# Where the first weight pieces are queued, who computes unit 1's own term, and a rewritten order: one change to a fused RWKV-5 / tanh-shrink kernel

## The chip, the cores and the metric

The kernel runs on one core of a Trainium2 chip. Time is device microseconds of one execution; the figure for a kernel is the median of its runs. A profile of one execution stands beside it: the hardware profiler records every instruction and every transfer. Engines: PE multiplies matrices (PEld loads its weights), DVE works on vectors, ACT evaluates functions and copies with a scale, POOL is the slow general engine, SP only issues transfers. ACT and POOL can issue transfers too.

## The reference

Two stages. The first is a linear recurrence over 768 steps for 4 batch rows and 8 heads of width 48:

```
for t in range(S):
    cur = u * k[t] (outer) v[t]              # the own term of step t
    y[t] = r[t] @ (state + cur)
    state = w * state + k[t] (outer) v[t]
```

The second takes y as x of 3072 x 384 (token by model width) through a dense block:

```
h = x @ w_in            # 384 x 2048
g = h - tanh(h)
out = g @ w_out         # 2048 x 384
```

r, k, v, w, u arrive as 32-bit floats. w_in and w_out arrive as 64-bit floats and are converted to 32 bits on the core, by integer and float operations on their two halves.

## The kernel before

**Units.** The recurrence is cut into 24 units, numbered 0 to 23. A unit is 64 steps of two batch rows, all 8 heads: r, k and v of a unit are six transfers of 96 KB (one per batch row and tensor). PE turns r and k (L656, four 128x128 transposes each), DVE scales them by powers of w out of the same PSUM tile into rT and kT (L660, L665; from the third unit on, kT is copied by ACT, L692), PE forms the products of all pairs of steps (`levels`, L606, `x_ps<-rT,kT`), DVE copies those that lie before the diagonal into `at` (L830), and PE multiplies `at` with v (`yk_ps<-at,vt`) and k with v for the state (`yk_ps<-vt,kw`). ACT copies the result to `xt` (L765); DVE or ACT keep the state (L792, L795). From the third unit on, the state enters by products `yk_ps<-rT,state` ahead of the levels.

**The own term** (the diagonal of `at`) is made in one of two ways. For units with n < OWN, ACT scales kT by w times u (`own_k`, L709, four instructions, needs `w_u` from POOL, L564), PE forms the products `x_ps<-rT,kU` (`own_levels`, 16 rows of PE's list, two matmuls each in the trace), and DVE copies their diagonal into `at` (L821). For the others, DVE multiplies r by k (L696) and by u (L824, needs `ub`), sums over each head (L700), and ACT writes the eight sums on eight diagonals (L704, two groups of four).

**Dense tiles.** Two units make a block of 256 tokens, 12 blocks. A tile is one block times 256 of the 2048 hidden columns: 96 tiles. PE makes h in two halves (L217, 1.29 us each), ACT and DVE turn it into g by five and three instructions (`s`, `th`, `tg`, `sq`, `small`; `g`, `m`, `cp`), and PE multiplies g by w_out: as four products (L254), or, from hidden column 1024 on for the first six blocks and for nearly all of the later ones, as seven half-width products of sums (L307), for which POOL adds parts of g (L290, L292, L294). The first six blocks run over the hidden columns in three passes (4, 4 and 8 groups of 128), so that they can begin with few weights.

**Weights.** The w_in and w_out matrices come in sixteen pieces of 768 KB, at first in the order w_in piece 0, w_in piece 1, w_out 0, w_out 1. A w_in piece is four transfers: two of 48 partition rows (288 KB) and two narrow ones of 16 rows (96 KB). Before the change the wide ones went by SP's queue and the narrow ones by POOL's. A piece is converted by five DVE instructions (L185, L186, L189, L190, L191) with two of ACT in between (L187, L188). The first h needs piece 0 after L191.

**What sets the order.** `lay_out` makes a list of some 2400 tasks (an engine, what must be done before, a cost and a due time). `ORDER`, a string of two-character numbers, then says in which order the tasks are written into the program; each engine executes its own in that order, waiting at an instruction until what it needs is there. Task numbers depend on the list, so another list needs another string. The tile framework adds the semaphore waits, also between two engines that only read one PSUM bank. Each transfer from SP or ACT counts on one of eight semaphores in turn (`DMAHW0` to `DMAHW7` in the rows below): a transfer that is issued eighth after another waits until that one has landed. The string also places filler matmuls (L534, on the identity matrix, results unused) where PE has nothing to do.

Of the kernel before, what the change touches and what calls it, by code (L numbers as in the profile page):

```python
# [34 lines left out]
OWN = 1  # L35
# [10 lines left out]
    "00010J2f2g2h2i2j2k2l2m2n0HbWbX02030K040605bWbWbW2o2q3534363231332r2t0I2s07370A0FbWbX080B0C2u2x2y38392v092w3U0D3C"  # L46
    "3B3V3W2p3A3G0U2z0L3R0M2+3S3T3D2_0N3F3H0V3Y0O3I0T3u3E3J0PbWbX3L3K3b0QbX3c300S3M3v3w3a0R3r3e3N3s3t3d0w3O3f3P3X3Z3g"
    "8D3Q3h3i3k0W0G3_4O3j0X8E0d430Y4P4Q3l4L0Z44404M4N453m8F0a3y463+0b3n413o0c423p3x3z15470ebYbYbY484p0u0E4Z8I4o4q0f8P"
    "4a0g494l0h4b4S4A4V4c0i4U4R4T4B3q4W0j8Q4m4n4C4X5I4v4Y4J5J5K4D8H4F0k4dbZ4e4K0l4I8L8R5F4G4f8G4H5G5H4z8SbZ4w134s8K8J"
    "4g5i8T8M8U4u4E4h8N4+8W4i4x8O8X8V4r4t4_8d4y4j5f505T0m525j5k510n5g5h5U8e0o8Y5L5V0p8p535M5N5W0q6C548g5P6D6E5X0r5O0t"  # L50
    "550s5Q698q5R5m565t6A6B8Z4k5S5A578h5lba5n595u8f5D5Y5p8i5B5v8j5C8a5Z5E5w6d8k8l5q6c6e8c5x5a6Z8m6N8b5o5b0v8n5r6a6b58"
    "145c6J8o6F5s5d6G6H8s6O775y8t6P6Q915z8r5e746R6n5+6o8u8w6I5_6j6K926L7678606p6g8x9D6M6373758v61666q688y6S6f6h676r64"
    "7W8z656T7X7Y9562946U937U98967T7V7H6i6V1D7I6k9E7J970xJ+996W9RJ_K06l6m796X7K0yJx9S6Y9H9F6s9I9J8+JyJz6t9T7A7B7h9G8_"
    "6u9K7L7D9A7C6vKP7EKM9d7F7G7a7i6w129e7j7Z7b906z6x7k9L6_KLKN9B6+7d9VKOKQ726y9WK9707M7l719C9X7N0z9M7cKA9U7O9f9YKu0+"
    "9Z7eKvKw7P9a9rKr7fK29i0_9N7Q1L7g7R9OKsKt9j16K1K3KZ9P177m9Q109h9g9b7n1811197o9l9k9s7p1ELF1F1TKBA17qKRL3LGLH9tKa7t"
    "9c1G7vKb7y9m9v7wA29w1A7u1H7x9z9n9xK61B9uLI9o9pLl9yA41CA5AFA3A81e1hKC1MLJLK1fAG1N9q1WKSKTA6KW1U1VAR1OA91g9+1PASAH"
    "1QAI9_A7L4AUAAA0AKAJAVANABKcAM1RALAfKD1SAgAT1I1xADLmLnAWAOACLoAYAjLpLqAZAiArAh7SAmAkAsAXL5AEAaB31iAv1jAtMAAP1J1k"
    "AnAwB41KAlAuAz1pAQAxAyM9MBB6AoBFA+B7LT1lBGBAB51mBTBH1nBIBJAb1XB81YMfB91oAcMgMh1ZBM2G2H1aBBBU2FBCBKBfAeBNBV1bBYBg"
    "Ad1cBXBWApBiBaBL1dAqBh1qBk2324KxA_1r26Bb251sKyKzBOB01t2E1yB1BjBt1z1u1+BuBm1_1vBZC3B2Bv1wByBDBcBw2P20BxC4BlB+BzBn"
    "BE27C5B_BP28Bo2921CH2AC82BBQC9C0C7CIC6BSBRCBBdCJCACM22BeCLCK2XCNCOCTKd2CBp2D2QBqCP2RCUBs2SCC2TChLzL+N4CWBrCXCiN3"  # L60
    "N52UCVCY2IC1CZCaCj2VCtCm2WCkC2CQCbClCDCnCpCoCE2JCq2KCuCF2LCGCcCRCw2MCvCyD52NCz2OCxD62YCS2ZD8C+D92aCdDCD7CeDACf2b"
    "DBDKCg2cDL7rC_DZD0DMDNDDDODa2dDP2eCrDbDRDcDe89CsDQDEDSD1DdDFDgDGDoDT85DUDp86DHEEDqDVDrDsEFDtDvDf87D2Du88EH81ETD3"
    "LUEUDhD4EGDwDIDiEVDxEJDjDJEIEKELDXDkEX8ADlEYEiEWDyEZEaDWEj8BDz8CD+ExEMEyENEbEmDYElEcE+82EkDmEpEOEn83E_FNEqEzF0Eo"
    "FOF3LVErDnFP84FQD_F2FSEd7sE1EeFRE0E2F1E3EPE4ERFTEQE5E6E7ESFVFUFcF4FdF5EsEgFgEtFeEfFfEhFhFjFrFiE8FWE9FsEBEAFkFXFl"
    "EvFuECFt7zFYFwG4FvEDFyFZG5F6FzEuEwG8F7FxGWFmG6F+G9FnF8G7GAGBFAGCF9FBFCGXF_FDGDG0GlGZFEFFFoGYFGGbFaFKGa7+Fb7_FHFp"
    "GeGE80GmFMGdFLFqGFGnFIGpG+GGGoG1GqFJGcG_GfG2GtH2GgGsH1GrG3H5GhH0GiGHGJH3GKGIGLH4GMHDGNGOGQHEGPGTH6HfK5HFH7HGGuGj"
# [328 lines left out]
def near(ctx, tc, r, k, v, w, u, out, shared, moe_w_in, moe_w_out):  # L395
# [3 lines left out]
    V, A, T, G, Q = nc.vector, nc.scalar, nc.tensor, nc.gpsimd, nc.sync  # L399
# [140 lines left out]
    def lay_out(early, across_by):  # L540
# [46 lines left out]
        for n in range(weights.count):  # L587

            queues, data = (("SP",), (3.0,)) if n % 4 > 1 else (("SP", "POOL") * 2, (1.2, .95) * 2)
            of = [add(e, .55, lambda n=n, i=i, e=e: weights.load(n, i, e_of[e]), [converted[n - 4] if n >= 4 else None],  # L590
                      data=x, gated=True) for i, (e, x) in enumerate(zip(queues, data))]
# [688 lines left out]
```

## Time and profile before

| | |
|---|---|
| median of 3 runs | 583.96 us (582.51 to 585.50) |
| profiled execution, its own time | 582.57 us |
| its span (first to last instruction) | 580.8 us |
| granted TensorE clock, mean | 0.998 |
| PE / DVE / ACT / POOL busy | 562.5 / 429.9 / 404.3 / 199.9 us |
| filler matmuls in PE's busy time | 13.5 us, all before 45.4 us |

Times in the rows are from the start of the span. A timeline row has start, busy time (us), engine, line of the program, operation, `out<-in`, count, and in brackets how long the engine had been idle before and what released it. `SPq`, `ACTq` and `POOLq` are the engines' issue queues. A windows row has the stretch, its length, then for each engine busy time (and instructions that began), then clock, share of the transfer engines and GB/s.

### The profile page before, as it was taken

The page shows a single profiled execution, that of the slowest core. Times are in us where ns is not written, and L with a number is a line of the kernel's source. Part 1 is how long each engine was busy: PE and PEld are TensorE (multiplying, and loading weights), DVE is VectorE, ACT ScalarE, POOL GpSimd, SP SyncE. Part 2 cuts the span into 40 slices and gives each one's busy share as a digit, 9 for nine tenths or more (in the row PEclk, how much of TensorE's full clock was granted, in tenths as well). Part 3 has the DMA queues.
Part 4 walks back from the last instruction along what each step waited for, and adds up shares of the span by engine and source line. Part 5 has one row for each costly group of instructions (what it writes and reads, how often), then busy time and mean ns, then how long its engine had stood idle before and what let it go on. Part 6 is the DMA issues. An engine that isn't in the chain of part 4 may idle for free.

```text
span 580.8 us, 14137 instructions
## 1 busy us (share of the span) xinstructions
PE 562.5 (97%) x5487; PEld 480.4 (83%) x5487; DVE 429.9 (74%) x720; ACT 404.3 (70%) x926; POOL 199.9 (34%) x366
## 2 busy tenths in 40 slices
PE   7699999999999999999999999999999999999995
PEld 4467777777776789999888889989999988999994
DVE  4899878999998787967699796567676766454534
ACT  2699999999977566545884787577577568765550
POOL 5201111300000233546256184273455253463430
PEclk9999999999999999999999999999999999999999
DMA  8987857594620000132344451441233000010001
GB/s 137 171 199 145 140 117 118 120 173 109 142 64 5 1 1 1 28 56 44 54 67 85 61 105 23 68 89 17 45 63 61 2 21 16 5 30 2 19 11 32
DMA packets 138549, 38.48 MB, mean 66 GB/s; under 512 B 130761, under 2 KB 132905, under 8 KB 138473
## 3 DMA queue, kind: packets, MB, share of 16 engines
q1 hardware_dynamic: 130140, 29.71, 28.7%
q0 software_dynamic: 4992, 6.99, 5.3%
q10 hardware_dynamic: 3340, 0.79, 0.9%
q8 instruction: 45, 0.74, 0.5%
q14 instruction: 32, 0.25, 0.2%
HBM read 31.66 MB, written 4.72 MB: 63 GB/s over the span
## 4 chain that ended last, share of the span: by engine, by line
PE 87%; DMA 4%; ACT 3%; DVE 2%; issue 1%; SPq 1%; POOL 0%; ACTq 0%; DVEq 0%; POOLq 0%
PE h L217 41%; PE p L307 26%; PE o L254 10%; PE yk_ps L606 6%; DMA rt<-in_r_dram 2%; PE x_ps L656 1%; DMA vt<-in_v_dram 1%; DMA xt<-rest 1%; ACT at L704 1%; PE x_ps L606 1%; SPq L644 1%; ACT xt L765 0%; PE p L254 0%; PE x_ps L534 0%; POOL xt L786 0%
## 5 line engine op out<-in xcount | busy, mean ns | idle before, releaser
L217 PE MATMUL h<-xt,w_in_sb 128*128 128x256 f32 x1152 | 267.3, 381 | 0.2 <-DMA xt<-rest 0.2
L217 PEld LDWEIGHTS h<-xt,w_in_sb 128*128 128x128 f32 x1152 | 214.9, 190 | 32.5 <-DVE g L242 1.5
L290 POOL TENSOR_TENSOR sg<-g 128x256 f32<-128x256 f32 x69 | 55.1, 800 | 197.7 <-DVE g L246 130.1
L242 DVE TENSOR_TENSOR g<-h,th 128x512 f32<-128x512 f32 x96 | 65.8, 686 | 67.9 <-ACT tg L233 25.2
L229 ACT ACTIVATE s<-h 128x512 f32<-128x512 f32 x96 | 57.1, 594 | 54.3 <-PE h L217 47.2
L307 PE MATMUL p<-mixed,sg 128*128 128x192 f32 x426 | 92.3, 327 | 0.0
L244 DVE TENSOR_TENSOR tg<-s,tg 128x512 f32<-128x512 f32 x96 | 69.3, 724 | 29.2 <-ACT s L224 19.4
L233 ACT ACTIVATE tg<-h 128x512 f32<-128x512 f32 x96 | 56.9, 594 | 41.9 <-PE h L217 29.9
L246 DVE COPY_PREDICATED g<-small,tg 128x512 f32<-128x512 int32 x96 | 72.0, 761 | 12.0 <-ACT small L235 9.0
L231 ACT ACTIVATE th<-h 128x512 f32<-128x512 f32 x96 | 56.7, 593 | 32.7 <-PE h L217 32.6
L307 PEld LDWEIGHTS p<-mixed,sg 128*128 128x128 f32 x426 | 73.3, 190 | 1.3 <-issue 0.3
L307 PE MATMUL p<-w_out_sb,g 128*128 128x192 f32 x284 | 70.4, 330 | 0.3 <-DVE o L335 0.3
L235 ACT ACTIVATE small<-s,smallb 128x512 f32<-128x512 f32 x96 | 68.5, 721 | 1.2
L254 PE MATMUL o<-w_out_sb,g 128*128 128x384 f32 x192 | 67.3, 489 | 0.0
L786 POOL DMA_DIRECT2D xt<-rest x66 | 32.5, 496 | 91.7 <-ACT rest L765 91.1
L224 ACT ACTIVATE s<-s 128x512 f32<-128x512 f32 x96 | 60.7, 633 | 1.4
L307 PEld LDWEIGHTS p<-w_out_sb,g 128*128 128x128 f32 x284 | 50.6, 190 | 3.1 <-DVE o L335 0.6
L254 PEld LDWEIGHTS o<-w_out_sb,g 128*128 128x128 f32 x192 | 35.8, 190 | 19.4 <-DVE parts L267 0.2
L704 ACT ACTIVATE at<-same,du 128x64 f32<-128x64 f32 x184 | 48.2, 342 | 0.5 <-DVE du L700 0.4
L292 POOL TENSOR_TENSOR sg<-sg,g 128x128 f32<-128x128 f32 x69 | 39.1, 569 | 3.1
L294 POOL TENSOR_TENSOR sg<-sg,g 128x128 f32<-128x128 f32 x69 | 37.2, 542 | 3.4
L307 PE MATMUL p<-mixed,g 128*128 128x192 f32 x142 | 34.7, 326 | 0.0
(127 smaller groups left out, 654.1 us busy)
## 6 DMA issues: line engine op xcount, KB each, us to landing
st<-in_moe_w_out_dram SPq DMA_DIRECT2D x8, 768.0 KB, 5.5
st<-in_moe_w_in_dram SPq DMA_DIRECT2D x16, 288.0 KB, 5.9
rt<-in_r_dram SPq DMA_DIRECT2D x46, 96.0 KB, 3.6
vt<-in_v_dram SPq DMA_DIRECT2D x46, 96.0 KB, 3.7
kt<-in_k_dram SPq DMA_DIRECT2D x44, 96.0 KB, 3.2
out_dram<-o POOLq DMA_DIRECT2D x44, 96.0 KB, 2.2
st<-in_moe_w_in_dram POOLq DMA_DIRECT2D x16, 96.0 KB, 5.9
parts<-in_k_dram SPq DMA_DIRECT2D x48, 32.0 KB, 2.1
```

The lines of the kernel that those rows point to most:

```text
L217: self.nc.tensor.matmul(t.h2[:, z], self.w_in_sb[:, t.f // 2, kk, z * 128 : (z + 1) * 128], self.xts[t.j][:, kk].rearrange("p b t -> p (b ...
L224: A.activation(t.s, t.s, AF.Square, scale=G3)
L229: A.activation(out, t.h, AF.Arctan, scale=G2)
L231: A.activation(out, t.h, AF.Tanh)
L233: A.activation(out, t.h, AF.Tanh, scale=G1)
L235: A.activation(out, t.s, AF.Relu, bias=self.smallb, scale=-1.0)
L242: V.tensor_tensor(t.g, t.h, t.th, ALU.subtract)
L244: V.tensor_tensor(t.tg, t.s, t.tg, ALU.mult)
L246: V.copy_predicated(t.g, t.small.bitcast(I32), t.tg)
L254: self.nc.tensor.matmul(self.outs[i], t.g2[:, z, i * C : (i + 1) * C], self.w_out_sb[:, t.f + z, :], start=t.first and z == 0, stop=t.last ...
L290: add(t.s4[:, :2], g[:, 0::3], g[:, 1:2].to_broadcast([128, 2, C]), ALU.add)
L307: self.nc.tensor.matmul(ps[bank][:, half * n : (half + 1) * n], a, b, start=t.first and half == 0, stop=t.last, skip_group_check=True)
```

## The change

Three things. `OWN` goes from 1 to 2: unit 1 makes its own term as unit 0 does, by products of PE. The narrow rows of the first two w_in pieces (n of 0 and 1 in the code, that is w_in 0 and w_in 1) are issued by SP instead of POOL, with 0.96 in place of 0.95 as their transfer cost in the list. And `ORDER` is another string throughout.

```
-OWN = 1
+OWN = 2
...
 ORDER = (
-    "00010J2f2g2h2i2j2k2l2m2n0HbWbX02030K040605bWbWbW2o2q3534363231332r2t0I2s07370A0FbWbX080B0C2u2x2y38392v092w3U0D3C"
...
+    "00012f2g2h2i2j2k2l2m2n0K0JbUbV020A030H0B040C2o320I06052q31333534362s072rbUbV082u2x2v2y2t3738392w0F09bV2z0L0M3P3A"
...
 def lay_out(early, across_by):
...
         for n in range(weights.count):
 
-            queues, data = (("SP",), (3.0,)) if n % 4 > 1 else (("SP", "POOL") * 2, (1.2, .95) * 2)
+            queues, data = (("SP",), (3.0,)) if n % 4 > 1 else (("SP", "SP" if n < 2 else "POOL") * 2, (1.2, .96 if n < 2 else .95) * 2)
```

The count of instructions changes little: 16 more products and 4 fewer filler rows on PE, on DVE one instruction each fewer of L696, L700 and L824 and one more of L821, on ACT eight fewer of L704 and four more of L709, and four transfers go from POOL's list to SP's. What moves is shown at three places, as pieces of the difference between the two programs' lists (a minus is the kernel before, a plus the change; the bracket holds the semaphores waited for).

SP's list, from its second transfer on (`st` is the staging tile of a weight piece, `rt_106`, `first_k_122`, `vt_116` are unit 0's r, k, v, and `rt_107`, `first_k_123` unit 1's):

```order
-L171 DMA st<-in_moe_w_in_dram 48x3x256
 L644 DMA rt_106<-in_r_dram 64x8x48
 L644 DMA first_k_122<-in_k_dram 64x8x48
-L644 DMA vt_116<-in_v_dram 64x8x48 [waits DMAHW0_49]
+L644 DMA vt_116<-in_v_dram 64x8x48
+L171 DMA st<-in_moe_w_in_dram 16x3x256 [waits DMAHW0_49]
 L171 DMA st<-in_moe_w_in_dram 48x3x256 [waits DMAHW1_49]
-L644 DMA first_k_123<-in_k_dram 64x8x48 [waits DMAHW4_49]
+L171 DMA st<-in_moe_w_in_dram 48x3x256 [waits DMAHW2_49]
+L171 DMA st<-in_moe_w_in_dram 16x3x256 [waits DMAHW3_49]
+L644 DMA rt_107<-in_r_dram 64x8x48 [waits DMAHW6_49]
+L644 DMA first_k_123<-in_k_dram 64x8x48 [waits DMAHW7_49]
```

Unit 0's r, k and v now go first; the whole of w_in piece 0 follows in four transfers, and unit 1 behind it. Further on in SP's list, unit 2's r and k come ahead of the wide rows of piece 1, and the first w_out transfer is row 31 instead of 24, the second row 34 instead of 38.

The start of ACT's and of DVE's list (`saved` is a copy of the turned w and u, from which POOL makes `w_u`; `by`, `power` and `inverse` are the powers of w and their reciprocals; `twice` feeds a table that ACT copies as `w_down`):

```order
-L560 ACT_TABLE_LOAD
+L563 ACT_TABLE_LOAD
+L563 COPY saved_157<-yk_ps_142 128x8 [waits PE_49]
+L644 DMA rt1_107<-in_r_dram 64x8x48 [waits DMAHW4_49]
+L644 DMA first_k1_123<-in_k_dram 64x8x48 [waits DMAHW5_49]
 L560 COPY twice_154<-inverse_153 128x512 [waits DVE_49]
-L563 COPY saved_157<-yk_ps_142 128x8 [waits PE_49]
```

```order
 L434 MEMSET plus 128x4 [waits DVE_49]
-L552 TENSOR_SCALAR by<-yk_ps 128x4x64 [waits PE_49]
+L552 TENSOR_SCALAR by<-yk_ps 128x4x64 [waits Activation_49]
 L554 SCALAR_TENSOR_TENSOR power<-by,plus 128x260 [waits DVE_49]
 L558 RECIPROCAL inverse<-power 128x260 [waits DVE_49]
```

ACT's table load and the copy `saved` stand ahead of two transfers and of `twice`, and DVE's `by`, which reads the same PSUM bank as `saved`, now waits for ACT where it waited for PE.

PE's list around the first tile of h (`kw_113` and `vt_117` belong to unit 1, `state_126` and `vt_118` to unit 2, `rt_106` here to unit 3):

```order
 L606 MATMUL yk_ps<-vt_117,kw_113 64x48 x16
-L217 MATMUL h<-xt,w_in_sb 128x256 x3
+L217 MATMUL h<-xt,w_in_sb 128x256 x6
 L606 MATMUL yk_ps<-rT,state_126 64x64 x16
 L606 MATMUL x_ps_146<-rT,kT 64x64 x16
-L217 MATMUL h<-xt,w_in_sb 128x256 x3
+L534 MATMUL x_ps_150<-ident 128x256
 L656 MATMUL x_ps_146<-ident,kw_113 128x128 x4
 L606 MATMUL yk_ps<-at_132,vt_118 64x64 x16
 L606 MATMUL yk_ps<-vt_118,kw_112 64x48 x16
 L656 MATMUL x_ps_146<-ident,rt_106 128x128 x4
-L534 MATMUL x_ps_150<-ident 128x512 x3
+L534 MATMUL x_ps_150<-ident 128x512 x2
```

The first tile's two halves (three rows each) stand together behind unit 1. Ahead of them, unit 1's own products come behind its levels. The turn of unit 2's r still stands ahead of unit 1's outputs, that of unit 2's k now behind them.

More of the change, by code (lines that the diff above doesn't have):

```diff
@@ L34 @@
 PASSES = 4, 4, 8
-OWN = 1
+OWN = 2
 SWAP = 2
@@ L86 @@
[L86 to L89 removed]
+    "00012f2g2h2i2j2k2l2m2n0K0JbUbV020A030H0B040C2o320I06052q31333534362s072rbUbV082u2x2v2y2t3738392w0F09bV2z0L0M3P3A"
```

89 lines of the change are left out of this document (44 added, 45 removed).

## Prediction

> **What bounds the kernel now.** I read the page's first part, then busy time by stretch, then the chain of waits of the start, then the timeline where the chain leads.
>
> ```profile
> span 580.8 us, 14137 instructions
> PE 562.5 (97%) x5487; PEld 480.4 (83%) x5487; DVE 429.9 (74%) x720; ACT 404.3 (70%) x926; POOL 199.9 (34%) x366
> DMA  8987857594620000132344451441233000010001
> 0.00:50.00 50.00, 40.41 (x756) 27.93 (x757) 38.16 (x70) 33.54 (x95) 14.18 (x47) 1.00 0.95 170
> 50.00:100.00 50.00, 48.59 (x929) 37.56 (x928) 42.09 (x76) 47.99 (x142) 8.63 (x18) 1.00 0.68 122
> 570.00:580.80 10.80, 4.74 (x22) 3.33 (x20) 3.25 (x8) 0.32 (x1) 0.00 (x0) 0.87 0.16 43
> 0.00:50.00 50.00, 13.51 (x30) 5.63 (x30) 1.00 0.95 170
> ```
>
> PE is busy for 97% of the span, so only less work or fewer holes can shorten it. The last row is the filler alone: of the first 50 us PE worked 40.41, but 13.51 of it is filler, so useful work is 26.9 and 23.1 us are lost. After that little is: 1.4 us from 50 to 100 (50 less 48.59), 6.1 in the last stretch, and of the 18.3 idle in all (580.8 less 562.5) the remaining 1.3 in between. The change adds a little PE work and rearranges mostly those 23.1 us, in a stage in which transfers are busy for 0.95 of the time at 170 GB/s.
>
> ```profile
> 4.19 6.26 DMA vt<-in_v_dram
> 8.30 0.60 SPq L644 DMA_DIRECT2D first_k<-in_k_dram  x1
> 15.20 7.33 DMA rt<-in_r_dram
> 22.66 0.63 PE L656 MATMUL x_ps<-ident,rt 128*128 128x128 f32 x4 [1.65 <-DMA rt<-in_r_dram]
> 23.22 0.58 PE L606 MATMUL yk_ps<-at,vt 64*64 64x64 f32 x24
> ```
>
> The two long links of the start's chain are transfers: unit 0's v (landing at 10.45), behind which SP cannot issue unit 1, and unit 2's r (22.53), whose turn stands in PE's list ahead of unit 1's outputs at 23.22.
>
> **The change, step by step.** At 170 GB/s, 96 KB take 0.58 us, 288 KB 1.73 and 768 KB 4.6.
>
> *Transfers.* Unit 0's six now lead; before, two wide ones and one narrow one (672 KB, 4.0 us) shared the engines with them. Between 0 (no sharing) and 4.0, I take 2.5: v lands near 8 and the issue of unit 1 goes on by then, where only its k could at 8.30. Unit 2's r: ahead of it and with it stand units 0 and 1 (1152 KB), piece 0 (768), `ub` (192) and r itself (192), 2304 KB or 13.9 us after the first data at about 2.9, so 16.8; before, unit 2's k, 288 KB and narrow rows came too, and it was 22.53. The first w_out piece has the same 4992 KB up to its end in both lists (before, POOL's early narrow rows of later pieces make up for it), about 33. Four more issues cost SP 4 x 0.6 = 2.4 us, in the gaps in which it waits for landings.
>
> ```profile
> 4.19 0.66 ACTq L644 DMA_DIRECT2D vt<-in_v_dram  x1
> 4.69 0.42 DVE L552 TENSOR_SCALAR by<-yk_ps 128x256 f32<-128x256 f32 x1 [2.54 <-PE yk_ps L549]
> 5.88 1.78 DVE L558 RECIPROCAL inverse<-power 128x260 f32<-128x260 f32 x1
> 8.37 1.28 ACT L560 ACT_TABLE_LOAD   x1 [8.37 <-DVE inverse L558]
> 9.64 0.68 DVE L665 TENSOR_TENSOR kT<-x_ps,inverse 128x512 f32<-128x512 f32 x1
> 10.19 0.16 ACT L563 COPY saved<-yk_ps 128x8 f32<-128x8 f32 x1
> 10.92 0.69 PE L606 MATMUL x_ps<-rT,kT 48*64 48x64 f32 x32
> 11.68 0.21 POOL L564 TENSOR_TENSOR w_u<-saved 128x4 f32<-128x4 f32 x1
> 12.23 0.97 ACT L709 ACTIVATE kU<-kT,w_u 128x128 f32<-128x128 f32 x3
> 13.66 0.75 DVE L821 COPY_PREDICATED at<-same,x_ps 128x512 f32<-128x512 int32 x1 [1.19 <-PE x_ps L606]
> ```
>
> *Unit 0.* Here the change adds a wait. `by` now comes behind ACT's `saved`, and that behind ACT's v issue (ends 4.85) and the table load (1.28): `saved` ends at 6.3, and `by`, `power`, `inverse` queued behind it on DVE end 1.65 later than before, at 9.3 instead of 7.66. kT waits for that; its transposes are long done. So kT starts at 9.35 (before 9.64), rT ends at 10.65, the levels start at 10.7 instead of 10.92: what the earlier transfers gained, the wait takes. But `w_u` is now ready by 7 and `kU` follows kT at once: 10.05 to 11.4, products to 11.7, masked copies on DVE to 12.85, before 14.41. **1.55 us** ahead.
>
> *Unit 1.*
>
> ```profile
> 18.41 2.02 ACT L704 ACTIVATE at<-same,du 128x64 f32<-128x64 f32 x8 [0.38 <-DVE du L700]
> 21.09 0.71 DVE L830 COPY_PREDICATED at<-before,x_ps 128x512 f32<-128x512 int32 x1
> 21.70 0.94 DVE L191 TENSOR_TENSOR w_in_sb<-w_in_sb,power 128x768 f32<-128x768 f32 x1
> 25.37 1.56 PE L217 MATMUL h<-xt,w_in_sb 128*128 128x256 f32 x6
> 30.39 1.56 PE L217 MATMUL h<-xt,w_in_sb 128*128 128x256 f32 x6
> ```
>
> Out go three DVE instructions of 0.55 and 2.02 us of ACT; in come 0.75 on DVE, 1.37 on ACT and 0.97 at most on PE. Unit 0's outputs take PE from 12.9 to 13.9, unit 1's turns 13.9 to 15.1, kT and rT DVE from 15.15 to 16.4, levels to 17.05, own products to 17.45 (kU 15.8 to 17.15). DVE copies the levels at 17.25, converts (L190), copies the diagonal 18.8 to 19.5; before, `at` was ready at 21.80. With unit 2's r long landed, the outputs start at 19.55, not 23.22: **3.7 ahead**. Piece 0: its last conversion stands behind two more DVE instructions for unit 2 and ends at 21.3 (before 22.64). After unit 1's state products PE starts h at 21.9 instead of 25.37 and does both halves in a row, to 24.6, where the second half ended at 31.95.
>
> *Units 2 to 6.*
>
> ```profile
> 30.60 0.74 DVE L830 COPY_PREDICATED at<-before,x_ps 128x512 f32<-128x512 int32 x1 [0.69 <-PE x_ps L606]
> 32.32 0.69 PE L606 MATMUL yk_ps<-at,vt 64*64 64x64 f32 x32
> 44.91 0.71 DVE L830 COPY_PREDICATED at<-before,x_ps 128x512 f32<-128x512 int32 x1
> 60.37 0.69 PE L606 MATMUL yk_ps<-rT,state 48*64 48x64 f32 x32
> ```
>
> Unit 2's levels follow h to 26.0; its copy on DVE starts at 26.05 (before 30.60), its outputs at 27.1 (before 32.32): 4.5 to 5.2 ahead. Then DVE's list has a product of the dense tile that needs ACT's `sq`, and ACT gets there only behind eight diagonals (2.02), the second table load (1.28), `s`, `tg`, `sq`: 28.1, so DVE stands 1.35 us. From unit 2's to unit 4's copy DVE took 14.3 us with hardly a pause. The change's stretch has 1.3 us less in it (conversions that come later), the stall of 1.35 and perhaps 0.4 for the w_out piece that lands near 33 while DVE wants it at 32.5: 14.8, so unit 4's copy comes near 41.0 instead of 44.91, **3.9 ahead**. Up to unit 6's state products both lists have the same tiles and units on PE; there the third tile's h waits 0.7 for a free PSUM buffer, and I get 57.2 against 60.37: **3.2 ahead**, with the added PE work already done inside what were holes.
>
> *The sum.* From there on PE is the bound and its work is the same, so I carry 3.2 to the end. 582.57 less 3.2 is 579.4 for an execution like the profiled one; the median of the runs lies 1.39 above that one, so **580.8** for the median. Bounds of what no row shows: the sharing of the first transfers (0 to 4.0, of which at most 1.5 reaches unit 0 since `inverse` holds kT), the landings of piece 1 and w_out (0 to 2 late), and how the new order fares after 60 us (below): 577.5 to 582.5.
>
> [...] The change leaves out three rows of filler before the first turn.
>
> ```profile
> L534 PE MATMUL h<-ident x20: 379/592/1219, 1.5 to 20.0; 128*128 128x512 f32 x12, 128*128 128x256 f32 x8
> ```
>
> The first filler took 1.22 us and a usual one 0.59, though the granted clock reads 1.00 throughout. [...]
>
> **Rivals.**
>
> *The products come too close behind h (slower).* In the order before, a tile's seven products stand on average 19 us of PE work behind its h, by my count over the list; in the new order, in the stage from about 220 to 400 us, often 6 to 12, and ten tiles have under 8 us (two did). Place: in block 7, PE's list has 12 rows of h for two tiles, then ten rows of other tiles' products, then the first tile's products. From the chain of waits a tile's h (12 matmuls, six rows) takes 2.59 us and a row of products (two matmuls of 28 in 4.55) 0.325, so the second tile's h and ten rows cover 5.8 us. What must fit in between stands below them:
>
> ```profile
> 251.16 2.59 PE h L217 x12
> 253.75 4.55 PE p L307 x28
> 464.44 1.56 PE L217 MATMUL h<-xt,w_in_sb 128*128 128x256 f32 x6
> 466.04 0.60 ACT L229 ACTIVATE s<-h 128x512 f32<-128x512 f32 x1 [5.62 <-PE h L217]
> 470.64 0.73 DVE L246 COPY_PREDICATED g<-small,tg 128x512 f32<-128x512 int32 x1
> 471.53 0.72 POOL L290 TENSOR_TENSOR sg<-g 128x256 f32<-128x256 f32 x1 [4.36 <-DVE g L246]
> ```
>
> From the end of h at 466.0 to the first sum at 472.25 it took 6.25 us, of which 1.05 were another unit's diagonals on ACT. So the point from which it decides is a cover of about 6 us where ACT or DVE serve a unit in between, 5.2 where not. If each of ten tiles stalls 0.65, that is 6.5 less the 3.2 gained: 587. Against it: a stall of one tile gives the next ones slack.
>
> *SP's line is too long (same).* Everything that units 1 to 5 need now stands in one queue with all of pieces 0 and 1 and, early, both w_out pieces; 30 rows are ahead of the first w_out, 23 before. If unit 3's v, behind 768 KB more, or unit 5's r (both w_out pieces ahead of it) lands 2.5 late, 0.7 remain: 583.3. For it: transfers at 0.95 already. Against: the bytes are those of before, and before, transfers fell to 0.82 from 33 to 48 us.
>
> ```profile
> 33.40:47.80 14.40, 13.57 (x304) 10.05 (x299) 14.17 (x25) 14.17 (x42) 3.43 (x7) 1.00 0.82 178
> ```
>
> [...]
>
> *It does not do what it says:* ACT's detour costs more than the own terms gain, if the table load starts late. Each microsecond there delays `inverse` by as much; at 3 late, 583.8.
>
> **How the numbers follow.** Lead kept: 0.60, 580.8 (own range 577.5 to 582.5). Lead given back in the transfers or behind the table load: 0.20, near 583.5. Products too close: 0.20, near 587. A difference of 0.5% (2.9 us) is about what a measurement of this kernel tells from none: faster means under 581.04, slower over 586.88. Of the first case I count 0.45 as faster and 0.15 as too small to tell, the second wholly as same; the third lies about its border, with a tail beyond that I give the whole 0.20. Range for 8 of 10: 577.5 to 587.
>
> **What would show it.** Right: unit 0's v lands by 8.5; `inverse` ends near 9.3 behind `saved`; unit 1's outputs start near 19.6 and the first h near 22, both halves together; unit 6's state products near 57; useful PE work in the first 50 us over 30. Wrong: `by` at 4.7 as before (then kT can come earlier and the gain is larger); an idle DVE at the conversions of piece 1 or w_out 0; PE idle of more than 3 us between 200 and 400, released by POOL's sums.

## The result and the profile after

| | before | the change |
|---|---|---|
| median of 8 runs | 581.12 us (580.63 to 585.50) | 587.91 us (583.06 to 592.50) |
| profiled execution, own time / span | 582.57 / 580.8 us | 585.14 / 583.3 us |
| granted clock in it, mean | 0.998 | 0.991 |

The ratio is 1.0084 (95% interval 1.0056 to 1.0112): slower by 0.8%, clear of the noise, and the median lies above the predicted range of 577.5 to 587. The ratio leaves out one slow run of the change (592.50 us). The page of the change, and its busy time by stretch (columns as in the prediction; the last row is filler alone):

```profile
span 583.3 us, 14226 instructions
PE 565.2 (97%) x5511; PEld 482.8 (83%) x5511; DVE 433.2 (74%) x718; ACT 404.9 (69%) x922; POOL 201.2 (34%) x362
DMA  7889484856400001313335454401440010010011
0.00:50.00 50.00, 41.57 (x781) 31.20 (x782) 36.49 (x67) 32.04 (x88) 12.12 (x43) 0.93 0.84 164
50.00:100.00 50.00, 48.17 (x919) 36.05 (x918) 42.73 (x77) 47.45 (x142) 8.79 (x18) 1.00 0.72 132
0.00:50.00 50.00, 11.33 (x22) 4.83 (x22) 0.93 0.84 164
```

In the first 50 us, idle and filler fell as forecast: 50 less 41.57 plus 11.33 is 19.8 us, before 23.1. But the clock of that stretch reads 0.93, so some of the busy time is the same work made longer: about 3.5 us of full-speed work (0.07 of 50) were not done in it, and the 3.3 gained are gone by 50 us.

The start of the change (timeline), in the order of the prediction's steps, and then two rows of the kernel before:

```profile
4.69 1.28 ACT L563 ACT_TABLE_LOAD   x1 [4.69 <-issue]
6.18 0.42 DVE L552 TENSOR_SCALAR by<-yk_ps 128x256 f32<-128x256 f32 x1 [4.03 <-ACT saved L563]
7.37 1.78 DVE L558 RECIPROCAL inverse<-power 128x260 f32<-128x260 f32 x1
10.54 0.26 POOL L739 COPY extra<-vt 128x96 f32<-128x96 f32 x1 [2.35 <-DMA vt<-in_v_dram]
5.61 1.11 PE L656 MATMUL x_ps<-ident,rt 128*128 128x128 f32 x4 [0.96 <-DMA rt<-in_r_dram]
8.19 2.77 PE L534 MATMUL h<-ident 128*128 128x512 f32 x4
11.74 1.02 PE L606 MATMUL x_ps<-rT,kT 48*64 48x64 f32 x32
20.16 0.69 PE L606 MATMUL x_ps<-rT,kU 48*64 48x64 f32 x32 [0.94 <-ACT state L795]
21.80 0.58 PE L606 MATMUL yk_ps<-at,vt 64*64 64x64 f32 x24
23.95 2.86 PE L217 MATMUL h<-xt,w_in_sb 128*128 128x256 f32 x12
28.04 0.73 DVE L830 COPY_PREDICATED at<-before,x_ps 128x512 f32<-128x512 int32 x1 [0.85 <-PE x_ps L606]
```

```profile
7.26 0.60 PE L656 MATMUL x_ps<-ident,rt 128*128 128x128 f32 x4
8.84 1.46 PE L534 MATMUL h<-ident 128*128 128x512 f32 x4
```

`inverse` ends at 9.15 behind `saved`. Unit 0's v lands near 10.5. Turn, filler and levels of unit 0 take 1.11, 2.77 and 1.02 us where the same rows before took 0.60, 1.46 and 0.69: PE is at about half speed, and gets out of it by the own products behind the levels (0.64 us for 32 matmuls, like the 0.69 before). The clock column does not show it: it reads 1.00 from 5 to 14 us. Unit 2's masked copy is at 28.04, 2.6 us ahead of before.

Then PE stands twice, and runs at half clock (timeline of PE, then one-microsecond stretches; below them two rows of the kernel before):

```profile
34.55 0.69 PE L606 MATMUL yk_ps<-rT,state 48*64 48x64 f32 x32 [1.69 <-DVE state L792]
36.94 1.13 PE L606 MATMUL yk_ps<-at,vt 64*64 64x64 f32 x32 [0.61 <-DMA vt<-in_v_dram]
43.72 0.69 PE L606 MATMUL yk_ps<-rT,state 48*64 48x64 f32 x32
36.00:37.00 1.00, 0.39 (x6) 0.09 (x5) 1.00 (x2) 1.00 (x6) 0.00 (x0) 0.70 0.89 165
37.00:38.00 1.00, 1.00 (x40) 1.00 (x44) 1.00 (x3) 1.00 (x5) 0.00 (x0) 0.50 0.71 133
42.00:43.00 1.00, 1.00 (x4) 0.82 (x3) 1.00 (x3) 1.00 (x2) 0.99 (x3) 0.50 0.75 145
43.00:44.00 1.00, 1.00 (x19) 0.58 (x22) 1.00 (x4) 1.00 (x3) 1.00 (x3) 0.88 0.72 143
```

```profile
39.15 0.69 PE L606 MATMUL yk_ps<-at,vt 64*64 64x64 f32 x32
43.56 0.69 PE L606 MATMUL yk_ps<-rT,state 48*64 48x64 f32 x32 [0.52 <-DVE state L792]
```

Granted clock (the third column from the right) is 0.5 from about 36.4 to 43.2. Unit 4's state products start at 43.72, before at 43.56: the lead of 2.2 us at unit 3's outputs (36.94 against 39.15) is used up. At unit 6's state products, which the prediction put at 57.2, the change is 0.5 us behind the kernel before (60.37):

```profile
60.90 0.69 PE L606 MATMUL yk_ps<-rT,state 48*64 48x64 f32 x32
```

The new wait comes later. In the third block (units 6 and 7) POOL sends six transfers of 16 KB that lay out unit 7's tokens (`xt<-rest`), and SP puts weight pieces in the same microseconds. First the change, then the kernel before:

```profile
76.33 0.96 POOL L786 DMA_DIRECT2D xt<-rest  x2 [14.50 <-ACT rest L765]
77.57 1.91 POOL L786 DMA_DIRECT2D xt<-rest  x4 [0.28 <-issue]
77.62 0.58 SPq L171 DMA_DIRECT2D st<-in_moe_w_out_dram  x1
78.25 0.47 SPq L171 DMA_DIRECT2D st<-in_moe_w_in_dram  x1
81.57 0.61 SPq L171 DMA_DIRECT2D st<-in_moe_w_in_dram  x1
84.14 0.67 PE L217 MATMUL h<-xt,w_in_sb 128*128 128x256 f32 x2 [0.97 <-DMA xt<-rest]
85.34 2.40 PE L217 MATMUL h<-xt,w_in_sb 128*128 128x256 f32 x10 [0.54 <-DMA xt<-rest]
```

```profile
73.41 0.57 SPq L171 DMA_DIRECT2D st<-in_moe_w_out_dram  x1
73.83 2.90 POOL L786 DMA_DIRECT2D xt<-rest  x6 [10.96 <-ACT rest L765]
80.95 4.05 PE L217 MATMUL h<-xt,w_in_sb 128*128 128x256 f32 x18
```

Before, one piece of 768 KB stands ahead of the small transfers, and h finds them landed (4.8 to 5.3 us after their issue). In the change 1344 KB are issued among them or just behind, they land 2.6 to 6.7 us after their issue, and the block's h waits 1.51 us. Other kernels with this rest of the order show more, below.

### The profile page after: what moved, and what is told of

Read it like the earlier page. It is cut to its first block, busy times and chain, and to the rows that moved or that the text cites. A ratio compares the mean times of both kernels' runs of the same rounds, so it can differ in the third digit from the quotient of the medians.

```text
span 583.3 us, 14226 instructions
## 1 busy us (share of the span) xinstructions
PE 565.2 (97%) x5511; PEld 482.8 (83%) x5511; DVE 433.2 (74%) x718; ACT 404.9 (69%) x922; POOL 201.2 (34%) x362
## 4 chain that ended last, share of the span: by engine, by line
PE 84%; ACT 5%; DVE 3%; DMA 3%; issue 1%; POOL 1%; SPq 1%; ACTq 0%; DVEq 0%; POOLq 0%
PE h L217 39%; PE p L307 27%; PE o L254 9%; PE yk_ps L606 6%; PE x_ps L656 1%; DMA vt<-in_v_dram 1%; DMA xt<-rest 1%; ACT at L704 1%; ACT th L231 1%; PE x_ps L606 1%; ACT tg L233 1%; SPq L644 1%; PE h L534 1%; DMA rt<-in_r_dram 1%; ACT s L229 1%
## 5 line engine op out<-in xcount | busy, mean ns | idle before, releaser
L290 POOL TENSOR_TENSOR sg<-g 128x256 f32<-128x256 f32 x69 | 53.0, 769 | 218.9 <-DVE g L246 160.9
L244 DVE TENSOR_TENSOR tg<-s,tg 128x512 f32<-128x512 f32 x96 | 71.6, 748 | 31.9 <-ACT s L224 18.5
L246 DVE COPY_PREDICATED g<-small,tg 128x512 f32<-128x512 int32 x96 | 73.4, 769 | 9.0 <-ACT small L235 4.3
L704 ACT ACTIVATE at<-same,du 128x64 f32<-128x64 f32 x176 | 45.6, 339 | 4.5 <-DVE du L700 4.4
L292 POOL TENSOR_TENSOR sg<-sg,g 128x128 f32<-128x128 f32 x69 | 41.2, 599 | 4.1
L294 POOL TENSOR_TENSOR sg<-sg,g 128x128 f32<-128x128 f32 x69 | 39.5, 576 | 4.0
L307 PE MATMUL p<-w_out_sb,sg 128*128 128x192 f32 x142 | 35.0, 328 | 0.2 <-POOL sg L294 0.2
```

What stands on the lines that cost most here:

```text
L244: V.tensor_tensor(t.tg, t.s, t.tg, ALU.mult)
L246: V.copy_predicated(t.g, t.small.bitcast(I32), t.tg)
L290: add(t.s4[:, :2], g[:, 0::3], g[:, 1:2].to_broadcast([128, 2, C]), ALU.add)
L307: self.nc.tensor.matmul(ps[bank][:, half * n : (half + 1) * n], a, b, start=t.first and half == 0, stop=t.last, skip_group_check=True)
```

## The experiments

Theory C: half clock takes the gain. Theory T: SP's longer list of transfers. Theory A: ACT's list (diagonals ahead of copies) stretches the units. Theory D: weight pieces against the small transfers. Theory N: the order, not the two small parts. Theory L and its rival S: the order behind about 55 us (the rest of the order, below), or ahead of it (its start). Theory O of the first four runs is the vague form of L. Each ratio is to the kernel before on the same chip.

**Filler against half clock.** PE's list (`warm_start` has the first plus, `warm_mid` the other two, `warm_both` all):

```
 L549 MATMUL yk_ps<-ident,rows 128x8
+L534 MATMUL h<-ident 128x512 x3
 L656 MATMUL x_ps<-ident,rt 128x128 x4        (unit 0)
...
-L534 MATMUL x_ps<-ident 128x512 x2
+L534 MATMUL x_ps<-ident 128x512 x4
 L606 MATMUL yk_ps<-rT,state 64x64 x16        (unit 3)
 L606 MATMUL x_ps<-rT,kT 64x64 x16
-L534 MATMUL x_ps<-ident 128x256
+L534 MATMUL x_ps<-ident 128x256 x2
```

> The change, with three more rows of 512-wide filler on PE ahead of unit 0's first turn, as the kernel before has them. Theory C (the change loses its lead because PE runs at half clock twice: in the start, where the turns, the filler and the levels of unit 0 took 1.11, 1.46 and 1.02 us instead of 0.60, 0.59 and 0.69, and again from 36.4 to 43.2 us, after a stall at 32.9): turns near 0.60 us, unit 0's levels start near 11.0 instead of 11.74 and its outputs near 13.8 instead of 14.92; the second stretch at half clock stays, since its stall lies behind ACT's diagonals, so about 1 us less than the change: near 587 if the change runs at 588. Theory T (transfers through SP's line are what is late): unit 0 is bound by v, which landed near 10.5, and by inverse, so the outputs move by less than 0.3 and the time stays at that of the change. Theory O (the later order, from 45 us on, costs the time): the time stays too, within 0.7.

> The change, with two more rows of 512-wide filler ahead of unit 3's levels and one more 256-wide row ahead of unit 3's outputs, where PE stood for 1.69 and 0.61 us. Theory C: the granted clock stays at 1.00 from 35 to 45 us, unit 4's state products start near 41 instead of 43.72, and the time is 3 to 3.5 us under that of the change, near 584.5, with a spread of its runs well under the 9 us of the change. Theory T: unit 3's v still lands at 36.9, the stall is only filled, and units 4 to 6 wait for their transfers: under 1 us gained. Theory O: unit 4 is earlier, but the lead is lost again by 120 us: under 1 us gained.

> The change with the added filler of both places (three 512-wide rows ahead of unit 0's first turn, two 512-wide ahead of unit 3's levels, one 256-wide ahead of unit 3's outputs). Theory C: the sum of both, 4 to 4.5 us under the change, near 583.5, and not slower than the kernel before by more than 0.5%. Theory T and theory O: within 1 us of the change, near 587.5.

Measured: 1.0076 (1.0044 to 1.0109), 1.0117 (1.0068 to 1.0165), 1.0103 (1.0070 to 1.0135). None is clearly better than the change. Of the three, `warm_mid` tests the stretch behind 36 us cleanly: in its profile the clock reads 1.00 up to 50 us, and it is no faster. In `warm_start` and `warm_both` unit 0 leaves half speed earlier (from 10 to 12 us PE begins 70 and 71 matmuls, in the change 15) and the clock reads 1.00 from 30 to 50 us, but half clock comes back between (0.76 and 0.88 from 16 to 30 us). The time went elsewhere, as the rows of PE in `warm_both` and the stretch behind them show:

```profile
83.52 0.67 PE L217 MATMUL h<-xt,w_in_sb 128*128 128x256 f32 x2 [0.68 <-DMA xt<-rest]
86.85 0.67 PE L217 MATMUL h<-xt,w_in_sb 128*128 128x256 f32 x2 [2.66 <-DMA xt<-rest]
87.86 3.06 PE L217 MATMUL h<-xt,w_in_sb 128*128 128x256 f32 x8 [0.34 <-DMA xt<-rest]
88.00:92.00 4.00, 4.00 (x52) 3.00 (x56) 0.00 (x0) 1.05 (x3) 0.00 (x0) 0.57 0.29 55
```

The third block's h waits 3.68 us here, and four microseconds at 0.57 of the clock follow. Theory C as the cause falls; in all three profiles half clock follows the waits for the third block, and from 80 to 130 us 1.7 us of full-speed work is lost to it in each.

**Transfers.** `narrow_pool` is the change with this line as before; `pieces_later` moves three rows of SP's list; `warm_pieces` is `warm_both` with that move:

```
-queues, data = ... (("SP", "SP" if n < 2 else "POOL") * 2, (1.2, .96 if n < 2 else .95) * 2)
+queues, data = ... (("SP", "POOL") * 2, (1.2, .95) * 2)
```

```
+L644 DMA kt<-in_k_dram 64x8x48
+L644 DMA rt<-in_r_dram 64x8x48 x2
+L644 DMA vt<-in_v_dram 64x8x48
+L171 DMA st<-in_moe_w_in_dram 48x3x256 x2
 L171 DMA st<-in_moe_w_out_dram 128x2x384
-L171 DMA st<-in_moe_w_in_dram 48x3x256
-L644 DMA kt<-in_k_dram 64x8x48
-L644 DMA rt<-in_r_dram 64x8x48 x2
-L171 DMA st<-in_moe_w_in_dram 48x3x256
-L644 DMA vt<-in_v_dram 64x8x48
```

> The change, but the narrow rows of the first two w_in pieces go by POOL's queue again (all else, the order too, as in the change). Theory T: SP's list is four transfers shorter ahead of unit 3, unit 3's v lands 1.5 us or more earlier than 36.9, and the time is 2 to 4 us under the change, near 585. Theory C: the stall at 32.9 comes from ACT, which has eight diagonals ahead of unit 2's copies, so the half clock stays and the time is within 1 us of the change. Theory O: the same, within 1 us.

> The change, with three rows of SP's list (the two wide rows of one w_in piece and one w_out piece, 1344 KB, issued at 77.6, 78.3 and 81.6 us) moved behind the third block's first h. Theory D (the third block's six small transfers from POOL, issued from 76.3 to 79.5 and landing up to 6.7 us later, share the engines with these pieces, and h waits for them at 83 to 86, by more in other executions): the transfers land within 4 us, PE has no wait on them between 80 and 90, the time is 3 to 4 us under that of the change (near 584.5) and its runs spread by less than 5 us. Theory A (the loss is made by 45 us, in ACT's list) alone: under 1.5 us gained. Theory C (half clock): nothing.

> The change with the filler of both places and with the three weight rows moved behind the third block's first h. In the run with the filler alone PE waited 3.7 us for the third block's transfers. Theory D: that wait falls under 0.7, and the time is 3 to 4.5 us under that of the run with filler alone, near 584. Theory A alone: within 1 us of it, since what the chain of units lost by 45 us is still lost. Theory C with D: another 2 us less than the three rows moved without the filler.

`narrow_pool`: 1.0102 (1.0054 to 1.0151), no gain, where theory T said 2 to 4 us; in the one profile (591.55 us, the second slowest of six) piece 0's last conversion starts at 24.18 instead of 22.46 and the first h at 27.04 instead of 23.95. Theory T falls; if anything, SP's narrow rows help the start in this order.

`pieces_later`: 1.0057 (1.0032 to 1.0083), `warm_pieces`: 1.0053 (1.0023 to 1.0083). Both lie below their counterparts (1.0084 and 1.0103), the second pair by 0.5%, though the intervals still touch. In both profiles no h waits for the third block's transfers. A third to a half seems to come back, less than theory D's 3 to 4 us, so D is probably a part of it; the other part stays (PE's idle time from 80 to 130 us in the profile of `pieces_later` is 2.76, no less than the change's 2.29). In `pieces_later` the kt of a unit lands late instead and DVE stands 2.32 us, and in `warm_pieces` it is the fifth block's turn:

```profile
88.29 0.56 DVE L696 TENSOR_TENSOR rk<-rt,kt 128x384 f32<-128x384 f32 x1 [2.32 <-DMA kt<-in_k_dram]
```

```profile
111.54 3.25 POOL L786 DMA_DIRECT2D xt<-rest  x6 [4.93 <-ACT rest L765]
111.95 0.62 SPq L171 DMA_DIRECT2D st<-in_moe_w_in_dram  x1
114.77 1.06 POOL L171 DMA_DIRECT2D st<-in_moe_w_in_dram  x2
120.34 9.74 PE L217 MATMUL h<-xt,w_in_sb 128*128 128x256 f32 x30 [2.79 <-DMA xt<-rest]
```

The same, from the other side: `before_pieces` is the kernel before with both wide rows of one w_in piece put behind its w_out row at 73.4.

```
 L171 DMA st<-in_moe_w_out_dram 128x2x384
+L171 DMA st<-in_moe_w_in_dram 48x3x256 x2
```

> The kernel before, with the two wide rows of the w_in piece that it issues later or earlier put right behind the w_out piece issued at 73.4 us, that is 576 KB more just ahead of the third block's six small transfers (issued 73.8 to 76.7). Theory D: they land 2 to 3.5 us later than the 5.8 us at most of before, PE waits for them near 82 us by 2 us or more, and the time is 2 to 4 us over that of the kernel before, with a wider spread of its runs (over 4 us). Theory A or C: within 1 us of the kernel before.

1.0035 (1.0007 to 1.0063): slower, at the lower edge of what D said. But PE's wait is not the one named. The small transfers land up to 7.6 us after their issue instead of 5.3; PE stands earlier, within a group of four transposes (first `before_pieces`, then before), so this run shows that 576 KB more at that place cost time, and not that they cost it by the wait of theory D (the last section has more on this wait):

```profile
82.74 0.33 PE L656 MATMUL x_ps<-ident,rt 128*128 128x128 f32 x1 [2.88 <-issue]
```

```profile
80.35 0.33 PE L656 MATMUL x_ps<-ident,rt 128*128 128x128 f32 x1 [1.18 <-issue]
```

**ACT's list.** `diag_later` moves eight diagonals each of units 3 and 4 behind the copies of the unit before. `split_pieces` is `pieces_later` with only the second group of four moved, behind the next kT:

```
-L704 ACTIVATE at<-same,du 128x64 x8
 L765 COPY xt<-yk_ps 64x3x64 x4
 L765 COPY rest<-yk_ps 64x64 x4
+L704 ACTIVATE at<-same,du 128x64 x8
 L692 COPY kT<-x_ps 128x512
```

```
-L704 ACTIVATE at<-same,du 128x64 x8
+L704 ACTIVATE at<-same,du 128x64 x4
 L765 COPY xt<-yk_ps 64x3x64 x4
 L765 COPY rest<-yk_ps 64x64 x4
 L692 COPY kT<-x_ps 128x512
+L704 ACTIVATE at<-same,du 128x64 x4
```

> The change, with the eight diagonals of units 3 and 4 on ACT (2.01 us each time) moved behind the copies of the unit before (xt and rest), which the next unit's state products wait for. Theory A: unit 2's rest ends near 32.2 instead of 33.9 and PE's stall of 1.69 us at 32.9 goes, unit 3's rest ends near 39 instead of 41.2, unit 4's masked copy on DVE comes near 42.5 instead of 44.95, and with the stall the half clock goes; the time falls by 2 us or more. Theory D: units 2 to 4 are earlier as said, but the third block's transfers meet the same weight pieces and the time falls by under 1.5 us.

> The change with the three weight rows behind the third block's first h, and the second of the two groups of diagonals of units 3 and 4 on ACT moved behind the next unit's kT (the first group stays ahead of the copies xt and rest), as the order before has it. Theory A with D: unit 2's rest ends 1 us earlier, unit 3's state products have no stall, unit 4's masked copy on DVE comes near 41.5 instead of 42.8 in the run with the rows moved alone, and the time is 1 to 1.5 us under that run, near 1.003 of the kernel before. Theory D alone (nothing before 45 us counts): within 0.7 us of that run.

1.0166 (1.0122 to 1.0210) and 1.0064 (1.0040 to 1.0089): the first clearly worse, the second no better than the rows moved alone. In `diag_later` unit 2's rest ended at 32.51, near the 32.2 forecast, and the stall shrank from 1.69 to 0.55 us, but kT now stood behind the diagonals:

```profile
33.16 0.69 PE L606 MATMUL yk_ps<-rT,state 48*64 48x64 f32 x32 [0.55 <-DVE state L792]
35.08 0.69 PE L606 MATMUL x_ps<-rT,kT 48*64 48x64 f32 x32 [1.23 <-ACT kT L692]
44.47 0.69 PE L606 MATMUL yk_ps<-rT,state 48*64 48x64 f32 x32 [2.27 <-ACT th L231]
```

In `diag_later` what is moved back makes the next thing late. In `split_pieces` the stall was 0.81 us, in `pieces_later` 0.96, so there the repair itself did little. Neither run bears theory A out; the cut below, where the start of the order before does not help, speaks against it more strongly.

**The small parts alone, in the order before.** The code lines are those of the change; `own_only` puts kU behind unit 1's kT, its products behind the levels, the copy behind that of the levels, and takes out the old term:

```
-OWN = 1
+OWN = 2
...
-L704 ACTIVATE at<-same,du 128x64 x8
+L709 ACTIVATE kU<-kT,w_u 128x128 x4
...
 L606 MATMUL x_ps<-rT,kT 64x64 x16
+L606 MATMUL x_ps<-rT,kU 64x64 x16
```

> The kernel before, with the narrow rows of the first two w_in pieces issued by SP at the places in the program where POOL issued them; the order is that of before. Theory N (the loss lies in the new order alone: what stands near what on SP, POOL and ACT from 28 us on): within 1 us of the kernel before. Theory T (SP's line is too long): unit 2's r lands 1 us or more after 22.5 and the time is 1.5 to 3 us over that of before.

> The kernel before with unit 1's own term made by PE's products (kU on ACT behind unit 1's kT, the products behind its levels, the masked copy behind that of the levels), and nothing else moved. Unit 1's outputs stand behind the turn of unit 2's r, which waits for its transfer until 22.66, so the 3.7 us of ACT and DVE work that it saves come in a stretch that waits for a transfer. Theory N: within 1 us of the kernel before, and unit 1's outputs still start near 23.2. A rival, that the own term itself costs (32 more matmuls and the copy of 0.75 us on DVE): 1 us or more over the kernel before.

> Both small parts of the change in the order of the kernel before: unit 1's own term by PE and the narrow rows by SP. Theory N: within 1 us of the kernel before, so 4 to 5 us under the change. Theory T or the rival that the own term costs: the sum of the two runs with one part, 2 to 4 us over the kernel before.

1.0012 (0.9985 to 1.0038), 1.0001 (0.9977 to 1.0024), 1.0001 (0.9984 to 1.0017). In `own_only` unit 1's outputs start at 23.22, as before to the hundredth: unit 2's r is what they wait for. Theory N stands: the new string is what costs the time.

**The order cut in two.** `new_then_old` has both small parts, the first 300 entries of the new `ORDER`, and from there the old order; `old_then_new` the reverse, cut at 306; `new_then_old_warm` adds the filler of `warm_mid`; `after_again` is the change once more. On SP the third block's stretch of the first then reads as in the kernel before:

```
-L171 DMA st<-in_moe_w_out_dram 128x2x384
-L171 DMA st<-in_moe_w_in_dram 48x3x256
-L644 DMA kt<-in_k_dram 64x8x48
...
+L644 DMA rt<-in_r_dram 64x8x48 x2
+L171 DMA st<-in_moe_w_out_dram 128x2x384
+L644 DMA kt<-in_k_dram 64x8x48 x2
```

> The two small parts of the change, the first 300 places of its order (up to about 55 us), and from there the order of the kernel before. Theory L (the loss is made between 60 and 130 us: POOL's six small transfers of the third and fifth block meet weight pieces there, and each wait for them is followed by 3.4 us at half clock): PE waits less than 1 us for these transfers, idle time from 80 to 130 us is 1 us as in the kernel before instead of 2.3 to 4.7, and the time is 0 to 3 us under that of the kernel before: in the first 50 us the change has 3.4 us less of idle and filler, of which a stretch at half clock can take all. Theory S (the loss is made before 55 us): 3 to 5 us over the kernel before, as the change.

> The two small parts of the change, the first 306 places of the order before (up to about 58 us), and from there the order of the change. Theory L: PE waits 2 us or more for the third or the fifth block's transfers, and the time is 3 to 5 us over the kernel before, like the change. Theory S: within 1 us of the kernel before.

> The same as the first of these four, with filler added ahead of unit 3's levels (two 512-wide rows) and outputs (one 256-wide), so that no half clock follows unit 2. Theory L with the half clock as the one that takes the lead at 36 to 43 us: granted clock 1.00 from 35 to 45 us and 2 to 3.4 us under the kernel before, better than both kernels. Theory S: 3 us or more over the kernel before.

> The change itself, once more, on the chip of these runs and with another execution profiled. Theory L: another 3 to 6 us over the kernel before, and where this execution is slower than the 585.14 of the first profile, the difference stands as PE's wait for the third or fifth block's transfers and the half clock after it, between 80 and 130 us. Theory S: the difference stands before 55 us.

1.0007 (0.9980 to 1.0033), 1.0085 (1.0056 to 1.0114), 0.9990 (0.9972 to 1.0008), 1.0099 (1.0069 to 1.0128). The old start with the new rest is as slow as the change; the new start with the old rest is not slower than before. The loss lies behind 55 us: theory L. The new start with the old rest is not faster than before either, with or without the filler, where theory L gave `new_then_old_warm` 2 to 3.4 us: the new start is worth nothing that shows in the time, even with the old rest behind it. The stretches agree on the loss; first `old_then_new`, then `new_then_old`:

```profile
80.00:100.00 20.00, 18.36 (x318) 13.63 (x316) 15.26 (x28) 18.05 (x52) 3.78 (x8) 1.00 0.74 143
100.00:130.00 30.00, 29.23 (x297) 21.48 (x296) 27.98 (x45) 27.47 (x61) 5.20 (x10) 1.00 0.73 179
```

```profile
80.00:100.00 20.00, 19.28 (x342) 14.84 (x344) 15.23 (x28) 18.81 (x57) 4.80 (x11) 1.00 0.52 116
100.00:130.00 30.00, 30.00 (x353) 21.98 (x344) 27.48 (x45) 29.56 (x70) 6.20 (x13) 1.00 0.77 139
```

PE's idle time from 80 to 130 us in the profiles (50 less the two busy times), with the clock's loss in that stretch (sum over two-microsecond stretches of 1 less the granted clock, times 2). The last column has the time from the start of unit 6's state products to the end of the span. Up to that row PE has done the same rows of h, products and turns in all of these profiles (48, 12 and 56, without filler), so the column is what the rest of the order takes:

| | idle 80 to 130 | lost to the clock there | from unit 6 to the end |
|---|---|---|---|
| old rest: before, `own_only`, `before_narrow`, `own_narrow`, `new_then_old`, `new_then_old_warm` | 0.6 to 0.8 | 0 | 518.6 to 520.4 |
| `before_pieces` | 2.7 | 0 | 521.0 |
| new rest: the change (twice), `old_then_new` | 2.3 to 2.5 | 0 | 520.9 to 523.0 |
| new rest: `warm_start`, `warm_mid`, `warm_both`, `narrow_pool`, `diag_later` | 3.3 to 4.7 | 0 to 3.4 | 522.9 to 526.9 |
| new rest, rows moved: `pieces_later`, `split_pieces`, `warm_pieces` | 2.8, 2.9, 5.1 | 0, 1.7, 3.4 | 522.1, 524.3, 528.1 |

Every profile with the new rest takes longer from unit 6 on than every one with the old rest as it was.

`after_again` could not show what its text asked for: the profiled execution was the fastest of seven (580.94 us; the median was 587.97), with a clock of 1.00 to the end. It shows the forecast almost as it was meant: idle and filler in the first 50 us of 19.7 instead of 23.1, third-block wait 1.60, unit 6's state products at 58.24, span 579.1, 1.7 under before:

```profile
58.24 0.69 PE L606 MATMUL yk_ps<-rT,state 48*64 48x64 f32 x32
```

**Two tries to beat both.** `new_then_old_warm2` adds three filler rows around unit 0's turns; `before_warm` adds filler to the kernel before:

```
+L534 MATMUL h<-ident 128x512 x2
 L656 MATMUL x_ps<-ident,rt 128x128 x4        (unit 0)
+L534 MATMUL h<-ident 128x512
 L656 MATMUL x_ps<-ident,first_k 128x128 x4
```

```
+L534 MATMUL h<-ident 128x512 x2
 L656 MATMUL x_ps<-ident,rt 128x128 x4        (unit 2)
...
+L534 MATMUL x_ps<-ident 128x512 x2
 L606 MATMUL yk_ps<-rT,state 64x64 x16        (unit 2)
```

> The kernel with the new start, the old rest and filler around unit 3 (0.999 of the kernel before), with three more 512-wide filler rows: two ahead of the turn of unit 0's r, one ahead of that of its k, so that PE does not enter unit 0 at half clock. If the half clock of the first 15 us reaches the end: unit 0's levels start 1 us earlier than 13.56 for the same landing of its r, and the time is 0.5 to 1.5 us lower, 0.996 to 0.998 of the kernel before. If the start is bound by the transfers of units 1 and 2: within 0.5 us, 0.998 to 1.000.

> The kernel before with filler where PE stood for 1.65 us (two 512-wide rows ahead of the turn of unit 2's r) and 2.2 us (two 512-wide rows ahead of unit 2's state products and levels). If half clock after these two waits is what spreads the executions of the kernel before (580.5 at a mean clock of 0.998, 585 at 0.990): the mean clock of its runs rises to 0.996 or more from 0.994 and the time falls by 1 to 1.5 us, 0.997 to 0.998. If not: within 0.3 us of the kernel before.

0.9989 (0.9974 to 1.0004) and 1.0015 (0.9995 to 1.0035). The first is as good as `new_then_old_warm` and not told apart from the kernel before. The second raised the mean granted clock of its runs to 0.997, from 0.995 of the kernel before on the same chip, and gained nothing: the half clock that this filler takes away cost nothing that shows. The profile of `before_narrow` says the same: it lost 3.4 us to the clock ahead of 50 us, and its span of 579.4 is shorter than that of the kernel before.

## Why the prediction was wrong

The lead over the kernel before, in us, at the points of the prediction's sum:

| point (time before) | forecast | the change | `after_again` |
|---|---|---|---|
| end of unit 0's masked copies (14.41) | 1.55 | -0.45 | 0.6 |
| unit 1's outputs (23.22) | 3.7 | 1.4 | 2.5 |
| unit 2's copy (30.60) | 4.55 | 2.6 | 3.7 |
| unit 4's copy (44.91) | 3.9 | 0.0 | 2.2 |
| unit 6's state products (60.37) | 3.2 | -0.5 | 2.1 |
| end of the span (580.8) | 3.2 | -2.5 | 1.7 |

Two steps failed: the lead was smaller than the sum at every point, and it was carried to the end through an order that takes longer.

**Transfers.** Unit 0's v was to land near 8 and landed near 10.5, before 10.45: the value taken (2.5) was wrong, the bound (0) right. Unit 2's r landed ahead of its turn, as said.

**Unit 0.** `by` behind `saved`, `inverse` near 9.3: right (9.15). Levels at 10.7: measured 11.74, 1.0 late, because the filler and the table ahead of them ran at half speed (2.77 against 1.46 us and 1.06 against 0.66, as the turn of r 1.11 against 0.60). The error was to put nothing into the sum for the slow first filler (1.22 us against 0.59) and the three rows of filler left out. In `after_again`, where the same 14 filler matmuls ahead of 30 us took 7.47 us instead of 7.69, the levels start at 10.92. A second error is in both executions: DVE's first masked copy was to follow the levels, and it began only behind the own products too (13.38 behind 13.24, and 12.28 behind 12.09).

**Unit 1.** Outputs forecast at 19.55, 3.7 ahead; measured 21.80, 1.4 ahead. One part is unit 0's lateness; another is a wait that the sum left out, in both executions: the own products stood 0.94 us behind ACT's `state` (L795). h came at 23.95 instead of 21.9, both halves together as said.

**Units 2 to 6.** Unit 2's copy at 28.04, 2.6 ahead of before (forecast 4.55). Unit 4's copy was to be at 41.0 and was at 44.95, before 44.91: from unit 2's copy DVE took 16.9 us, not 14.8. PE's stalls of 1.69 and 0.61 were in none of my terms, and the half clock of 36.4 to 43.2 followed them. In `after_again` the same kernel stood 1.25 and 0.30 us there and had no half clock; so this term is there in one execution and not in another, and the lead at unit 6 is 2.1 in one and gone in the other, not 3.2.

**"From there on PE is the bound and its work is the same, so I carry 3.2 to the end."** This is the step that decided. The work is the same, but PE is not the bound all the way: in the new rest its h waits for transfers. The cut shows it: with the old rest 1.0007, with the new rest 1.0085. From unit 6's state products on, the kernel before took 520.4 us, the change 522.4 and 520.9: the rest was to cost nothing and cost 2.0 and 0.5 us in the two profiles, and 0.8% or more, that is over 4 us, in the ratios. The prediction looked at the new order between 200 and 400 us, in PE's rows, and not at POOL's small transfers against SP's pieces between 70 and 120 us, though it named transfers as the scarce thing itself.

**The step to the median.** The 1.39 us from the profiled execution to the median came from three runs. With eight, the median of the kernel before is 581.12, 1.45 us below that execution, so 580.8 for the change would have been a gain of 0.3 us over it, not of 3.2.

**Rivals.** "Products too close behind h" gave 587 and the median came at 587.9, by luck, since the mechanism was another: PE's idle time from 200 to 400 us was 0.47 us (before 1.20), not 6.5. "SP's line is too long" had the right kind of cause, a transfer that lands late, but at units 3 to 5, where it cost 0.61, and with SP's longer list as its reason, which `narrow_pool` and `before_narrow` rule out. "It does not do what it says" did not happen.

**What stays open.** The profiled executions of the change are the second fastest of 8 and the fastest of 7. From 80 to 130 us they show 1.7 and 1.9 us more idle time than before, while the medians differ by 5 to 7 us. That executions nearer the median lose the other part in longer waits for the blocks' transfers with half clock behind them is what the profiles of `warm_start`, `warm_mid` and `warm_both` suggest (3.3 to 4.7 us idle and 1.7 to the clock); no such execution of the change itself was profiled. Half clock alone is not enough for it: executions of the change took 589.35 and 589.23 us at a mean clock of 0.996, where 0.4% of the time is 2.4 us. Which rows of the new rest cost what, beyond the three that were moved, was not settled.

## What to carry to other kernels

A lead in the start is worth only what is left of it further on and what the rest of the order can keep. Compare two orders at a row up to which both have done the same work: it tells apart what the start gained and what the rest lost. When an order is rewritten, look for each small transfer that the critical engine waits for, at which big ones are issued in the few microseconds around it, to the end of the loading stage. To find what in a large rewrite costs the time, cut the order: the first part of one with the rest of the other, both ways, told at once what repairs of single places had not. And where PE waits a microsecond or two in a stretch that it bounds, count the half clock behind it as a possible second price, here of another 1.7 us (`warm_both`) to 3.4 us (`warm_pieces`) from 80 to 130 us.

## What the runs showed of the hardware that was not expected

**Half clock after short waits.** In the change no single wait of PE ahead of the drop at 36.4 us was longer than 1.69 us; from 33.0 to 36.4 PE was busy for 1.8 of 3.4 us: the stretch ahead of the drop was half idle, no more. Such a stretch does not always go with a drop: the kernel before stood 2.21 us from 27.6, busy for 0.79 of the 3 us from 27 to 30, and `warm_start` waited 1.7 us for the same `state`, busy for 0.46 of the 2 us from 34 to 36, and in both the clock reads 1.00 there and in the ten microseconds behind it. What decides between the two is not shown.

**Executions differ by the clock.** Over 129 executions of the kernel before, on the chips of these runs, the 20 with a mean granted clock of 0.998 or more have a median of 581.0 us, the 13 with 0.990 or less 585.0. Which of the two causes the other is not shown.

**A wait for nothing that the profile shows.** In the kernel before PE stands 1.18 us between the third and the fourth transpose of one group, put down to `issue`; with 576 KB more in the queues (`before_pieces`) it was 2.88, and with other instruction counts (`own_only`, `own_narrow`) it is not there. The traces list transfers of kind `instruction`; those of 16 KB are on queue q8. The other such wait of the kernel before, and the one transfer of q8 in the stretch from 27 to 28.5 us:

```profile
29.77 0.69 PE L606 MATMUL x_ps<-rT,kT 48*64 48x64 f32 x32 [2.21 <-issue]
q8 instruction: 1, 0.02, 5.1%
```

It landed at 28.36, 1.41 us ahead of the end of the wait; another landed at 79.05, 1.30 us ahead of the end of the wait of 1.18 us. Waits of PE of more than 1 us that are put down to `issue` stand in other kernels too, from 1.24 us (`before_narrow`) to 2.88 (`before_pieces`). Most of the 45 transfers of q8 in the kernel before have no such wait behind them: it has two. Whether PE waited for these transfers is not shown: no run moved one.
